# Last output tile: each store as two transfers of 64 rows, one from SyncE and one from ScalarE

## The chip, the cores and the metric

The kernel runs on one core of one Trainium2 chip. The metric is the device time of one execution in microseconds, as the median of several runs. In the text TensorE, VectorE, ScalarE, GpSimd and SyncE are the five engines of the core; the profile calls them PE, DVE, ACT, POOL and SP. SyncE computes nothing: it waits for semaphores and issues transfers (DMAs) between the core's memory (SBUF) and the chip's (DRAM).

## What is computed

For an input x of 2048 rows with 448 columns the kernel computes a gated mix of two branches:

```
g   = sigmoid(x @ gate_w)                        # one number per row
a   = attention(x @ wqkv) @ wo                   # 16 heads of 28; each row looks at 8 rows, 2 apart
b   = relu(x @ w1 + b1)**2 @ w2 + b2             # 448 -> 1792 -> 448
out = g * a + (1 - g) * b
```

Everything is float32. Matrix products are made from a high and a low part of each operand, in three products.

## The kernel before, in words

The 2048 rows are split by parity (`par` 0 and 1), since the attention steps by two, and each parity into eight tiles of 128 rows (`t` 0 to 7). Four chunks of four such tiles go through the matrix products of q, k and v (lines 257 to 298). Then the four chunks go through the other branch in the order 3, 0, 1, 2 (line 50 and the loop at line 1049), while GpSimd and VectorE work on the attention beside it. The order on every engine is written out by the program itself: `advance` (line 478) keeps a planned clock of TensorE and calls what has come due.

A finished tile of the output comes together in SBUF in `bt` tiles of 128 rows by 448 columns. `fin_add` (line 822) adds one branch's sum, scaled by its gate, to such a tile: one VectorE instruction (line 823), then a transfer. If the other branch was already there, the tile goes to the output (line 825); otherwise it goes to a buffer in DRAM (line 831) or is kept. All transfers are issued by SyncE, in the order in which the program asks for them. A transfer counts up one of eight completion semaphores in turn, and the next transfer on the same semaphore first waits for it.

The last work is the product with `wo` for the tiles 6 and 7 of parity 1, in `wo_last` (line 926). Its helper list `outs` has three entries: tile 6 with all 448 columns (r = 0), tile 7 with the first 224 columns, and tile 7 with the last 224 (both r = 1). For each entry nine matmuls run (line 944), then `fin_add` adds and stores (line 946). So the last tile is stored in two halves of 224 columns, 112 KB each, and the second can be issued only when the last nine matmuls and VectorE's add behind them are done. Other lines that the prediction speaks of: 367 (o_d stores of 128 rows), 639 (the first load of the program), 642, 876 and 1004 (loads of 64 rows), 571 (ScalarE's one-column copies).

At the end of the program (line 1165 in the profile) SyncE waits for all completion semaphores and for the other engines' counters, in five waits of two semaphores each. Then all engines meet in a barrier.

Of the kernel before, what the change touches and what calls it, by code (L numbers as in the profile page):

```python
# [13 lines left out]
S, D, H, DH, W, F = 2048, 448, 16, 28, 8, 1792  # L14
P = 128
# [42 lines left out]
def gated_mix_kernel(ctx: ExitStack, tc: tile.TileContext, xT, wqkv, w1, w2, wo, b1, b2, out):  # L58
    nc = tc.nc
# [38 lines left out]
    zt, gt, g1t = zg[:, 0:2], zg[:, 2:4], zg[:, 4:6]  # L98
# [46 lines left out]
    def ps(tag, name):  # L145
        return psum.tile([P, 512], F32, tag=tag, name=name, bufs=4)
# [331 lines left out]
    def advance(dt):  # L478
        clock["pe"] += dt
        while due := [x for x in later if x[0] <= clock["pe"]]:  # L480
            item = min(due, key=lambda x: x[0])
            later.remove(item)
            item[1]()
        if not clock["on"]:
            clock["att"] = clock["pe"]
            return
        while clock["att"] < clock["pe"]:
            try:
                r = next(att)
            except StopIteration:  # L490
                clock["on"] = False
                return
            if r is None:
                clock["att"] = clock["pe"]
                return
            clock["att"] += r
# [300 lines left out]
    fin = {}  # L797
# [21 lines left out]
    def fin_tile(par, t):  # L819
        return ahead.pop((par, t), None) or fin_begin(par, t)  # L820

    def fin_add(par, t, bt, pt, g, cols=slice(0, D)):
        nc.vector.scalar_tensor_tensor(bt[:, cols], pt, g, bt[:, cols], op0=ALU.mult, op1=ALU.add)  # L823
        if (par, t) in fin:
            nc.sync.dma_start(out[par, t, :, cols], bt[:, cols])
            fin[par, t] = "stored"
        elif par == 1 and t < 4:
            ahead[par, t] = bt
            fin[par, t] = "half"
        else:  # L830
            nc.sync.dma_start(f_d[par, t], bt)
            fin[par, t] = "half"
# [3 lines left out]
    def o_part(c, f, second, tls):  # L836

        for tl in tls:
            if f == 0 and not second:
                bps[tl] = Acc("b", f"b{c}_{tl}", D, 6 * NF)  # L840
        todo = []
        for r in range(2):
            tl = tls[(r + f // 2 + second) % 2]
            sl = slice(tl * P, tl * P + P)
            ps = []
            for g in (f + 1, f) if second else (f, f + 1):
                (hh, hl), (wh, wl) = hs[c, g], w2hl(g)
                ps += [(bps[tl], a[:, sl], w) for a, w in (((hl, wh), (hh, wh), (hh, wl)) if second else
                                                           ((hh, wh), (hh, wl), (hl, wh)))]
            todo.append(ps)  # L850
        go(todo, MM448)
        if second and f == NF - 2:
            for tl in tls:
                par, t = c // 2, (c % 2) * 4 + tl
                fin_add(par, t, fin_tile(par, t), bps[tl].pt[:, :D], g1t[:, par, t:t + 1])
# [56 lines left out]
    def wo_three(acc, oh, ol, wh, wl):  # L912
        return [(acc, oh, wh), (acc, oh, wl), (acc, ol, wh)]

    def wo_full(st, r, ks):
        _, _, accs, oh, ol, *_ = st
        return sum((wo_three(accs[r], oh[:, k, r], ol[:, k, r], woh[:, k], wol[:, k]) for k in ks), [])
# [8 lines left out]
    def wo_last(st, between):  # L926


        par, t, accs, oh, ol, o7, o8 = st
        half = D // 2  # L930
        outs = [(0, accs[0].pt, slice(0, D)), (1, accs[1].pt, slice(0, half)),
                (1, ps("b", "last"), slice(half, D))]
        for j, (_, a, w) in enumerate(wo_three(None, o7, o8, wo7h, wo7l)):
            for r, pt, cols in outs:
                rows = slice(r * 64, r * 64 + 64)
                nc.tensor.matmul(pt[:, :cols.stop - cols.start], a[rows], w[rows, cols], start=j == 0, stop=False)  # L936
        advance(3 * MM448)
        between()
        tiles = [fin_tile(par, t + r) for r in range(2)]
        for r, pt, cols in outs:  # L940
            n = cols.stop - cols.start
            todo = wo_full(st, r, (0, 1, 2))
            for j, (_, a, w) in enumerate(todo):
                nc.tensor.matmul(pt[:, :n], a, w[:, cols], start=False, stop=j == len(todo) - 1)  # L944
            advance(9 * MM448 * n / D)
            fin_add(par, t + r, tiles[r], pt[:, :n], gt[:, par, t + r:t + r + 1], cols)

    def wo_second(st):
        par, t, accs, *_ = st
        go([wo_full(st, 1 - r, (2, 0, 1)) for r in range(2)], MM448)  # L950
        for r in range(2):
            fin_add(par, t + r, fin_tile(par, t + r), accs[r].pt[:, :D], gt[:, par, t + r:t + r + 1])
# [161 lines left out]
    for n, (tls, second) in enumerate(((left, False), (right, False), (left, True), (right, True))):  # L1114
        if second:
            o_turn(c, f, tls)
        if n in (1, 2, 3):
            st = at_hand()
            if n == 3:
                wo_last(st, lambda: o_part(c, f, second, tls))  # L1120
                break
            split_now()
            wo_first(st)
        o_part(c, f, second, tls)
        if n in (1, 2):
            wo_second(st)
# [43 lines left out]
```

## Time and profile before

| | us |
|---|---|
| median of 3 runs | 415.18 (414.21 to 415.46) |
| the profiled execution | 414.58 |
| its span, first to last instruction | 412.7 |
| end of the last matmul, from the start of the span | 409.64 |
| issue of the last store begins | 410.14 |

The profile is of one execution. Its times count from the start of the span; the 1.9 us between span and execution lie around it. A row of a transfer (DMA_DIRECT2D, engine SPq) shows how long its issue kept SyncE, not how long the data moved; "to landing" counts from the start of the issue until the completion semaphore has its full count. The granted clock of TensorE was 1.00 throughout.

### The profile page before, as it was taken

To read this page: it belongs to the slowest core of one execution; us is meant where nothing else is said; L and a number is where in the kernel's file an instruction comes from. 1 tells how busy PE (TensorE), PEld (TensorE's weight loads), DVE (VectorE), ACT (ScalarE), POOL (GpSimd) and SP (SyncE) were. 2 spreads that over 40 slices of the span, in tenths; PEclk is the share of its full clock that TensorE was granted. 3 is DMA by queue.
4 is the path that set the end of the run, shared out by engine and by line. 5 is a ranking of instruction groups with operands and counts; after the bars stand their busy time and mean duration, and the time that the engine had idled before them with its cause. 6 is when DMAs were issued, how large, how long until landed. Compare 5 with 4: busy or idle time off the path is not lost.

```text
span 412.7 us, 9323 instructions
## 1 busy us (share of the span) xinstructions
PE 408.4 (99%) x3835; PEld 377.6 (91%) x3835; DVE 255.9 (62%) x404; ACT 211.9 (51%) x477; POOL 268.6 (65%) x167
## 2 busy tenths in 40 slices
PE   8999999999999999999999999999999999999997
PEld 8999999999999999888888888989898888888996
DVE  4520523276767767777656798879576677892354
ACT  5642556378756565444565535444653254346540
POOL 0000000965989999999989899999899977860000
PEclk9999999999999999999999999999999999999999
DMA  7989799989164307654112649765145611168204
GB/s 236 380 318 326 227 364 292 363 259 321 47 224 159 128 2 258 207 186 152 37 50 93 233 157 266 200 149 149 24 163 192 224 46 59 72 175 139 91 0 180
DMA packets 65611, 73.76 MB, mean 179 GB/s; under 512 B 32352, under 2 KB 58528, under 8 KB 65184
## 3 DMA queue, kind: packets, MB, share of 16 engines
q1 hardware_dynamic: 65568, 73.16, 54.5%
q8 instruction: 30, 0.49, 0.5%
q14 instruction: 13, 0.11, 0.1%
HBM read 45.71 MB, written 28.25 MB: 179 GB/s over the span
## 4 chain that ended last, share of the span: by engine, by line
PE 99%; DVE 0%; issue 0%
PE b L188 33%; PE h L188 32%; PE qkv L188 23%; PE a L188 7%; PE qkv L266 2%; PE warm L632 1%; PE a L944 1%; PE last L944 0%; DVE bt L823 0%; PE last L936 0%; PE a L936 0%; DVE zero L629 0%; DVE b1z L630 0%
## 5 line engine op out<-in xcount | busy, mean ns | idle before, releaser
L339 POOL TENSOR_TENSOR qk<-q,k 128x896 f32<-128x896 f32 x64 | 135.0, 2138 | 83.2 <-DMA k<-k_d 78.9
L346 POOL TENSOR_TENSOR av<-lg,v 128x896 f32<-128x896 f32 x64 | 119.5, 1962 | 8.0 <-DVE lg L340 5.6
L188 PE MATMUL qkv<-wqh,x 64*128 64x448 f32 (+1 forms) x528 | 90.9, 360 | 0.0
L619 DVE TENSOR_TENSOR h<-h,h 128x512 fp32r<-128x512 f32 x56 | 38.3, 687 | 60.8 <-ACT h L622 60.4
L188 PEld LDWEIGHTS qkv<-wqh,x 64*128 64x128 f32 x528 | 74.0, 184 | 1.3
L188 PE MATMUL qkv<-wql,x 64*128 64x448 f32 (+1 forms) x264 | 74.7, 360 | 0.0
L188 PE MATMUL b<-w2ah,h 64*128 64x448 f32 x448 | 70.4, 359 | 0.0
L188 PE MATMUL b<-w2bh,h 64*128 64x448 f32 x448 | 69.6, 360 | 0.0
L340 DVE TENSOR_REDUCE lg<-qk 128x32 f32<-128x896 f32 x64 | 67.1, 1076 | 2.2 <-POOL qk L339 2.1
L354 DVE TENSOR_REDUCE o<-av 128x112 f32<-128x896 f32 x64 | 66.5, 1070 | 2.1 <-POOL av L346 1.8
L620 ACT ACTIVATE h<-h,b1z 128x512 f32<-128x512 f32 x56 | 36.7, 656 | 44.0 <-PE h L188 44.0
L188 PEld LDWEIGHTS b<-w2ah,h 64*128 64x128 f32 x448 | 48.0, 184 | 2.8
L188 PEld LDWEIGHTS b<-w2bh,h 64*128 64x128 f32 x448 | 46.0, 184 | 3.2 <-ACT h L571 0.3
L188 PE MATMUL b<-w2al,h 64*128 64x448 f32 x224 | 47.6, 358 | 0.0
L188 PEld LDWEIGHTS qkv<-wql,x 64*128 64x128 f32 x264 | 45.5, 184 | 0.7
L188 PE MATMUL b<-w2bl,h 64*128 64x448 f32 x224 | 45.8, 358 | 0.0
L207 ACT ACTIVATE st<-qkv 128x448 f32<-128x448 f32 x48 | 24.5, 543 | 32.2 <-PE qkv L188 27.1
L188 PE MATMUL h<-x,w1h 64*128 64x512 f32 x168 | 36.1, 386 | 0.0
L621 ACT ACTIVATE h<-h 128x512 fp32r<-128x512 f32 x56 | 33.5, 599 | 1.7
L622 ACT ACTIVATE h<-h 128x512 f32<-128x512 f32 x56 | 33.2, 593 | 0.0
L188 PE MATMUL h<-x,w1l 64*128 64x512 f32 x84 | 29.7, 386 | 0.0
L571 ACT ACTIVATE h<-h 128x4 fp32r<-128x4 f32 (+1 forms) x35 | 7.2, 206 | 42.6 <-PE b L188 42.4
(145 smaller groups left out, 749.4 us busy)
## 6 DMA issues: line engine op xcount, KB each, us to landing
k<-k_d SPq DMA_DIRECT2D x8, 840.0 KB, 6.7
v<-v_d SPq DMA_DIRECT2D x8, 840.0 KB, 4.4
x_d<-x SPq DMA_DIRECT2D x11, 512.0 KB, 6.0
q_d<-st SPq DMA_DIRECT2D x8, 448.0 KB, 4.6
k_d<-st SPq DMA_DIRECT2D x8, 448.0 KB, 4.1
v_d<-st SPq DMA_DIRECT2D x8, 448.0 KB, 7.1
w1raw<-w SPq DMA_DIRECT2D x4, 896.0 KB, 10.0
q<-q_d SPq DMA_DIRECT2D x8, 448.0 KB, 3.6
```

Source lines behind the costliest of these rows:

```text
L188: nc.tensor.matmul(acc.pt[:, :acc.n], a[rows], w[rows], start=acc.todo == acc.all, stop=acc.todo == 1)
L207: nc.scalar.activation(st[:, :, t % 2], pt[:, :D].rearrange("p (g c) -> p g c", g=G), AF.Copy)
L266: nc.tensor.matmul(acc.pt[:, :NQ], a, w, start=k == j == 0, stop=False)
L339: nc.gpsimd.tensor_mul(pr, q[:, s:s + 1].to_broadcast([P, W, C]), k[:, s:s + W])
L340: pending.append(lambda: nc.vector.tensor_reduce(lg[:, s], pr.rearrange("p w (h d) -> p w h d", h=HG), axis=AX.X, op=ALU.add))
L346: nc.gpsimd.tensor_mul(pr.rearrange("p (h d) w -> p w h d", h=HG), lg[:, s][:, :, :, None].to_broadcast([P, W, HG, DH]), v[:, s:s + W].rea ...
L354: nc.vector.tensor_reduce(o[:, g * C:(g + 1) * C], pr, axis=AX.X, op=ALU.add)
L571: nc.scalar.activation(ap, f32(ap), AF.Copy)
L619: nc.vector.tensor_sub(hl, pt, f32(hh))
L620: ops += [lambda pt=pt, r=r: nc.scalar.activation(pt, pt, AF.Relu, bias=b1t[:, f + r:f + r + 1]), lambda pt=pt, hh=hh: nc.scalar.activatio ...
L621: lambda pt=pt, hh=hh: nc.scalar.activation(hh, pt, AF.Square),
L622: lambda pt=pt, r=r, low=low: (nc.scalar.activation(pt, pt, AF.Square), at(delays[r], low))]
```

## The change

`fin_add` gets a flag, `two`. `wo_last` passes `r`, so that it is set for the two column halves of tile 7 and for nothing else. With the flag, the store of a half goes as two transfers: rows 0 to 63 issued by SyncE and rows 64 to 127 issued by ScalarE, 56 KB each. The rest of the program is as it was.

```diff
-    def fin_add(par, t, bt, pt, g, cols=slice(0, D)):
+    def fin_add(par, t, bt, pt, g, cols=slice(0, D), two=False):
         nc.vector.scalar_tensor_tensor(bt[:, cols], pt, g, bt[:, cols], op0=ALU.mult, op1=ALU.add)
-        if (par, t) in fin:
+        if two:
+            for e, rows in ((nc.sync, slice(0, 64)), (nc.scalar, slice(64, P))):
+                e.dma_start(out[par, t, rows, cols], bt[rows, cols])
+            fin[par, t] = "stored"
+        elif (par, t) in fin:
             nc.sync.dma_start(out[par, t, :, cols], bt[:, cols])
             fin[par, t] = "stored"
...
-            fin_add(par, t + r, tiles[r], pt[:, :n], gt[:, par, t + r:t + r + 1], cols)
+            fin_add(par, t + r, tiles[r], pt[:, :n], gt[:, par, t + r:t + r + 1], cols, r)
```

## The prediction

> **What bounds the kernel now.** I read four views of the profiled execution of the kernel before, from the outside in: the page for the whole span, the chain that ended last for its last microseconds, the timeline of the same stretch, and SyncE's own waits.
>
> ```profile
> span 412.7 us, 9323 instructions
> PE 408.4 (99%) x3835; PEld 377.6 (91%) x3835; DVE 255.9 (62%) x404; ACT 211.9 (51%) x477; POOL 268.6 (65%) x167
> PE 99%; DVE 0%; issue 0%
> ```
>
> TensorE (PE) is busy for 408.4 of 412.7 us and 99% of the chain runs on it. The change touches no matmul, and the order of instructions on TensorE, VectorE and GpSimd is the same in both kernels. So nothing can be won or lost but in what follows the last matmul. The chain of the last 8 us, and the timeline from 409.5 us, show where that begins:
>
> ```profile
> 408.62 1.02 PE last L944 x9
> 409.64 0.02 issue
> 409.66 0.45 DVE bt L823
> ...
> 410.14 0.33 SPq L825 DMA_DIRECT2D out<-bt  x1
> ```
>
> In the first three rows the columns are start, length, what. The last matmul ends at 409.64, VectorE adds its result into the output tile until 409.66 + 0.45 = 410.11, and SyncE (SP) begins to issue the last store at 410.14. The chain as printed stops at 410.11, because it follows instructions and not transfers; the span goes on to 412.7. Those last 2.6 us are the whole field of this change. What SyncE waits for in them (total, times, longest), and how busy the 16 DMA engines are (last two columns: their share, and GB/s):
>
> ```profile
> SPq L1165 <- DMA out<-bt: 0.8, 1, 0.8
> SPq L1165 <- PEq L1165: 0.6, 2, 0.4
> ...
> 410.45:410.95 0.50, 0.00 (x0) 0.00 (x0) 0.00 (x0) 0.00 (x0) 0.00 (x0) 1.00 0.00 0
> 410.95:411.50 0.55, 0.00 (x0) 0.00 (x0) 0.00 (x0) 0.00 (x0) 0.00 (x0) 1.00 0.66 209
> 411.50:411.95 0.45, 0.00 (x0) 0.00 (x0) 0.00 (x0) 0.00 (x0) 0.00 (x0) 1.00 0.05 18
> ```
>
> So the tail has five pieces: the issue (0.33), a gap without traffic until about 410.95, the packets until about 411.5, their confirmation until the landing at 410.14 + 1.7 = 411.84 (the 1.7 is quoted below), and then the closing barrier of all engines up to 412.7. SyncE waits 0.8 us for that store with nothing else to do: the landing of the last store sets the end.
>
> **The change part by part.** The output tile for r = 1 is stored in two column halves. I call them A (first 224 columns, begun at 409.1) and B (last 224 columns, begun at 410.14). Each now goes as two transfers of 64 rows: A1 and B1 from SyncE, A2 and B2 from ScalarE. By the order lists SyncE still issues two transfers there, ScalarE two more, each behind one wait.
>
> *The issue.* Rows of all transfers of a line: least, median, longest duration in ns, first and last start. The first two lines move 128 rows per transfer, the last three 64 rows.
>
> ```profile
> L367 SPq DMA_DIRECT2D o_d<-o x16: 319/320/602, 230.9 to 369.6; - x16
> L825 SPq DMA_DIRECT2D out<-bt x17: 332/338/1357, 270.5 to 410.1; - x17
> ...
> L1004 SPq DMA_DIRECT2D woraw<-wo_d x2: 497/542/587, 189.4 to 189.9; - x2
> L642 SPq DMA_DIRECT2D wqraw<-wqkv x2: 572/579/586, 4.0 to 4.6; - x2
> L876 SPq DMA_DIRECT2D ot<-o_d x16: 612/617/837, 248.0 to 380.1; - x16
> ...
> SPq L1004 <- ACT h L621: 0.4, 1, 0.4
> ...
> L825 SPq DMA_DIRECT2D out<-bt x1: 332/332/332, 410.1 to 410.1; - x1
> DMA to landing us min/median/max: 1.7/1.7/1.7
> ```
>
> Half the rows doesn't mean half the issue: all 20 transfers of 64 rows took 0.50 to 0.84 us to issue, while a store of 128 rows takes 0.32 to 0.34 as a rule. The nearest row is the 0.497: it is a 64-row transfer that, like B1, came straight after a wait for a compute engine (the wait is the row of L1004 on ScalarE's h); the others stood in a rush of issues. I take 0.50 in place of 0.33: **+0.17 us**. From below, if the cost went with the rows, it would be 0.17 instead of 0.33, −0.17; from above, with the longest row, 0.84, +0.50. Nothing hides this: the issue begins when VectorE is done and the packets follow it. For A1 and A2 it is hidden: they begin at 409.1 and B at 410.14, so an issue of up to about 0.97 us is covered by VectorE's wait for the last matmuls and its add; above that, B starts late by the excess.
>
> ScalarE has issued no transfer in the trace of before. Its last instruction is long done:
>
> ```profile
> 400.88 0.19 ACT L571 ACTIVATE h<-h 128x2 fp32r<-128x2 f32 x1
> ...
> L639 SPq DMA_DIRECT2D wqraw<-wqkv x1: 391/391/391, 0.7 to 0.7; - x1
> ...
> L825 SPq DMA_DIRECT2D out<-bt x1: 1357/1357/1357, 404.5 to 404.5; - x1
> DMA to landing us min/median/max: 3.5/3.5/3.5
> ```
>
> No work of ScalarE stands behind A2 and B2, so nobody waits for what is queued there but the closing barrier. The bounds for an issue by ScalarE are 0.33 (a 128-row store of SyncE) and 1.36 (the longest store issue in this trace). I take SyncE's 0.50, because SyncE's very first issue, the second row, cost only 0.39: a queue's first use is not dear there. The waits put ahead of the four transfers are for earlier transfers that used the same completion semaphore. The latest of those is the store issued at 404.5, which lands 3.5 us later at 408.0, a microsecond before A begins: 0.
>
> *The packets.* Two sizes of 128-row stores have a time to landing:
>
> ```profile
> out<-bt SPq DMA_DIRECT2D x15, 224.0 KB, 2.0
> out<-bt SPq DMA_DIRECT2D x2, 112.0 KB, 1.7
> ```
>
> Half the bytes land 0.3 us earlier; halving once more, to 56 KB, would give about 0.15. That is the most that smaller transfers can win. But B1 and B2 come out together and the same 112 KB must be moved: the 0.66 share between 410.95 and 411.50 is all 16 DMA engines at work on them. I take **0**, with −0.15 as the other end. The Trainium skill, page "DMA: Bandwidth & Descriptors", section "Rules for kernel authors", speaks against this change: two transfers to disjoint halves of the partitions serialise, since both spread over the same engines, whether one engine issues them or two, so one 128-partition transfer is better. By it this term is 0, as taken; by the two sizes alone it would be −0.15. No run here shows two queues at once.
>
> A moves too: its packets come about 0.17 later, into the stretch from 410.45 to 410.95, whose share of 0.00 shows that it is free.
>
> *The closing waits.* Before the barrier SyncE checks all completion semaphores in five waits:
>
> ```profile
> L1165 SPq EVENT_SEMAPHORE  x5: 27/28/28, 410.5 to 411.9; - x5
> ...
> L1165 SPq EVENT_SEMAPHORE  x3: 27/28/28, 410.9 to 411.0; - x3
> ...
> L1165 SPq EVENT_SEMAPHORE  x1: 28/28/28, 411.9 to 411.9; - x1
> ```
>
> Before, four pass between 410.5 and 411.0 while the last store is under way, and only the fifth, at 411.9, is held by it. In the changed program B1's and B2's semaphores are named in the second and third wait, so two or three waits are left to pass after the landing. The three from 410.9 to 411.0 make two steps in some 0.1 us, about 0.07 a step: two or three steps are 0.14 to 0.2. I take **+0.15**, with 0 and 0.3 as ends. What follows (the barrier, 0.8 us) is unchanged.
>
> *The sum*: +0.17 + 0 + 0.15 = +0.32 us, rounded to +0.35 for the second issuer. The profiled execution took 414.58 us, of which 1.9 lie around its span of 412.7; with the change 414.93. The median of the three runs, 415.18, is 0.60 above the profiled one, so I forecast **415.5 us** for the median. 0.3% of this kernel is 1.25 us, which is also what its three runs spread over (414.21 to 415.46): about what a measurement can tell from no change. The forecast is **no change that can be told**.
>
> **The rivals.**
>
> *The two issues take turns.* If SyncE and ScalarE cannot generate transfers at the same time, B2 starts when B1's issue is over. For it: back-to-back issues on SyncE never overlap. Against it: those are one engine's, and no row shows two. Price: a second 0.50 in line, less the 0.15 because the last train is then half as long: +0.35 more, in all +0.7, 415.9 us. The Trainium skill, page "Perfetto Trace Analysis", section "DMA Instruction — HWDGE (DVE, Sync)", says that the block that generates descriptors is shared between issuing sequencers and locked for one at a time; by that this rival would be the case, and no run here shows it.
>
> *The halves do win.* The issue costs no more than before (0.33) and each train is half as long: −0.15 and the closing waits +0.15, in all 0; with the issue at half, −0.17: 415.0 to 415.2. Against it: 20 of 20 rows with 64 rows are slower to issue.
>
> *ScalarE is a slow issuer* (the other side: slower). The mechanism is two ScalarE issues of length I in line, A2 from about 409.14 and B2 behind it. Up to I = 0.96 A2 is covered and only B2 counts: I − 0.33. Above, B2 ends at 409.18 + 2I in place of 410.47, so 2I − 1.29, less 0.15 for the half train, plus 0.15 for the closing waits. It costs more than 1.25 us from I = 1.27 on; at the 1.36 row it is +1.43, 416.6 us, and at 1.6 it would be +1.9, 417.1. For it: nothing in the trace shows ScalarE issue, and SyncE itself has issues that long. Against it: the median of SyncE's 17 stores is 0.34.
>
> *It doesn't do what it says* is as good as excluded by the order lists; left is a shift in the program's code that moves some wait unseen.
>
> **How the numbers follow.** The forecast (both halves side by side, 415.2 to 415.8) has 0.42; the issues in turn 0.20; the halves win 0.12; the slow ScalarE 0.24; anything else 0.02. Slower by over 0.3% (above 416.4): most of the slow ScalarE, 0.20, and 0.08 from the two milder losses where the spread of runs adds to them: 0.28. Faster by over 0.3% (below 413.9): no case reaches it, since from the end of the last add to the landing there are only 1.7 us and at most 0.3 of them could go; 0.05 for the spread of runs. Within 0.3%: 0.67. The range goes from 414.3 (the best case, −0.3, in a run as quick as the quickest shown) to 417.0 (the slow ScalarE nearly to its end).
>
> **What would show it.** Right, if the profile after has issues of 0.45 to 0.65 us for both B1 and B2, begun within 0.1 us of each other; one train of packets of about 0.5 us beginning some 1.0 us after the issue begins; a landing 0.1 to 0.25 us later than the 1.7 of before; and two or three of SyncE's five closing waits after it. Wrong, if B2's issue begins or ends after B1's by the length of an issue (turns), if a row of ScalarE shows over 1.2 us (slow issuer), if the landing comes before 1.7 us (the halves win), or if anything before 409 us moved.

## The result, and the profile after

| | before | after |
|---|---|---|
| median of 22 runs each, us | 414.56 (414.11 to 415.86) | 415.49 (414.9 to 417.69) |
| ratio to before | 1 | 1.0024 (95% interval 1.0016 to 1.0033) |
| the profiled execution, us | 414.58 | 415.25 |

The change costs about 1.0 us (0.7 to 1.4 by the interval). With 22 runs of each kernel that is clear of no change, though it is below 0.3%.

The page of the kernel after shows four instructions more (two waits and two transfers of ScalarE) and a second queue, q10, ScalarE's, beside SyncE's q1. Its columns are packets, MB, and share of the DMA engines.

```profile
span 413.5 us, 9327 instructions
...
q10 hardware_dynamic: 160, 0.11, 0.1%
```

The 160 packets are two transfers of 64 rows with 16 completion marks each. The end of the chain of the kernel after (start, length, what):

```profile
408.55 1.02 PE last L949 x9
409.57 0.02 issue
409.59 0.45 DVE bt L823
```

The last add ends at 409.59 + 0.45 = 410.04, against 410.11 before. In these two executions nothing was lost ahead of the last store; the tail behind the last add grew from 2.61 to 3.43 us. Its first piece, the two issues of half B:

```profile
L827 SPq DMA_DIRECT2D out<-bt x1: 496/496/496, 410.1 to 410.1; - x1
L827 ACTq DMA_DIRECT2D out<-bt x1: 511/511/511, 410.1 to 410.1; - x1
```

They stand side by side, half a microsecond each, and begin 4 ns apart; the one before took 0.332. The landings, from the DMA page of the same stretch (last column, us after the issue began):

```profile
out<-bt SPq DMA_DIRECT2D x1, 56.0 KB, 1.9
out<-bt ACTq DMA_DIRECT2D x1, 56.0 KB, 2.3
```

The store of before took 1.7 to land. Both halves are later than that, with half the bytes, and ScalarE's is later by 0.35 than SyncE's, although both issues ran at the same time. The packets say why. From 411.19 to 411.48 only SyncE's queue moves:

```profile
q1 hardware_dynamic: 55, 0.05, 75.4%
```

from 411.49 to 411.64 both move:

```profile
q10 hardware_dynamic: 26, 0.02, 60.4%
q1 hardware_dynamic: 22, 0.01, 21.2%
```

and from 411.66 to 411.93 ScalarE's queue and a code load (q14, kind instruction):

```profile
q10 hardware_dynamic: 47, 0.03, 48.2%
q14 instruction: 1, 0.01, 10.1%
```

The second transfer starts in its turn, 0.28 behind the first, and is still under way when the first is done; the issue rows show nothing of it. This late start is what the text calls a turn. Behind the landing, SyncE's closing waits:

```profile
L1170 SPq EVENT_SEMAPHORE  x3: 28/28/299, 412.1 to 412.5; - x3
L1170 SPq DRAIN  x2: 7/7/7, 412.5 to 412.6; - x2
```

The 299 ns is the wait that ScalarE's landing ends (at 412.34); two more follow. Last, the barrier. ScalarE's DRAIN in the kernel after, and in the kernel before:

```profile
L1170 ACTq DRAIN  x1: 135/135/135, 413.1 to 413.1; - x1
```

```profile
L1165 ACTq DRAIN  x1: 14/14/14, 412.3 to 412.3; - x1
```

Before, it began 0.1 us after the ScalarE wait ahead of it (412.2); after, 0.35 later than its wait (412.8), and all engines waited for it.

For all kernels of this study, from the records of the traces, in us after the end of the last add: when the first data packet of each queue's part of half B starts, when the last part has landed, and then how long the closing waits and the barrier took. Landing, closing waits and barrier add up to the tail. Of x1, x2, x3 and x7 to x10 there is one execution each, the profiled one, so that only the tail is used of them.

| kernel | SyncE's packets | ScalarE's packets | last landing | closing waits | barrier | tail |
|---|---|---|---|---|---|---|
| before | 0.85 | | 1.76 | 0.09 | 0.76 | 2.61 |
| after | 1.17 | 1.45 | 2.29 | 0.19 | 0.94 | 3.43 |
| x1: rows 0-63 by SyncE alone | 1.22 | | 2.05 | 0.09 | 0.76 | 2.90 |
| x2: rows 64-127 by ScalarE alone | | 1.24 | 2.74 | 0.09 | 0.76 | 3.59 |
| x9: rows 0-63 by ScalarE alone | | 1.24 | 2.73 | 0.09 | 0.76 | 3.58 |
| x3: both by SyncE | 1.49, 2.31 | | 3.17 | 0.25 | 0.76 | 4.18 |
| x7: 16 columns of B | 1.18 | 1.45 | 2.04 | 0.19 | 0.94 | 3.18 |
| x6: only B in halves | 1.22 | 1.50 | 2.35 | 0.09 | 0.76 | 3.20 |
| x4: halves by columns | 0.85 | 1.00 | 1.81 | 0.19 | 0.94 | 2.94 |
| x5: B whole by ScalarE | | 0.90 | 1.84 | 0.09 | 0.76 | 2.69 |
| x8: after, two copies more | 1.18 | 1.45 | 2.23 | 0.19 | 0.76 | 3.18 |
| x10: before, four copies more | 0.85 | | 1.73 | 0.09 | 0.94 | 2.76 |
| x12: both cut 96 and 32 | 0.84 | 1.18 | 1.99 | 0.19 | 0.94 | 3.12 |
| x11: only B cut 96 and 32 | 0.87 | 1.21 | 2.01 | 0.09 | 0.76 | 2.86 |

After against before: landing +0.54, closing waits +0.10, barrier +0.18, together +0.82.

### The profile page after: what moved, and what is told of

The parts are those of the page before. It is cut to its first block, busy times and chain, and to the rows that moved or that the text cites. A ratio compares the mean times of both kernels' runs of the same rounds, so it can differ in the third digit from the quotient of the medians.

```text
span 413.5 us, 9327 instructions
## 1 busy us (share of the span) xinstructions
PE 408.1 (99%) x3835; PEld 374.9 (91%) x3835; DVE 255.9 (62%) x404; ACT 211.9 (51%) x477; POOL 268.4 (65%) x167
## 4 chain that ended last, share of the span: by engine, by line
PE 97%; DMA 1%; SPq 0%; DVE 0%; ACT 0%; issue 0%
PE b L188 33%; PE h L188 32%; PE qkv L188 23%; PE a L188 7%; PE qkv L266 1%; DMA xraw<-xT 1%; PE a L949 1%; PE last L949 0%; SPq L644 0%; SPq L639 0%; DVE bt L823 0%; ACT x L662 0%; PE last L941 0%; PE a L941 0%
## 5 line engine op out<-in xcount | busy, mean ns | idle before, releaser
L188 PE MATMUL b<-w2bh,h 64*128 64x448 f32 x448 | 68.6, 360 | 0.0
L188 PE MATMUL b<-w2bl,h 64*128 64x448 f32 x224 | 44.9, 358 | 0.0
L188 PE MATMUL h<-x,w1h 64*128 64x512 f32 x168 | 35.2, 386 | 0.0
L188 PE MATMUL h<-x0b,w1h 64*128 64x512 f32 x168 | 28.1, 386 | 0.0
```

Source lines behind the costliest of these rows:

```text
L188: nc.tensor.matmul(acc.pt[:, :acc.n], a[rows], w[rows], start=acc.todo == acc.all, stop=acc.todo == 1)
```

## The experiments

Three theories for the late landing: **G**, the two transfers take turns where transfers are generated (a descriptor, in the expectations, is the order for one packet); **E**, they take turns because the DMA engines or the memory's ports are busy with the first one; **S**, ScalarE's queue is slower by itself. Diffs are against the changed kernel, inside `if two:`, unless another kernel is named.

### x1: rows 0 to 63 by SyncE alone

```diff
-            for e, rows in ((nc.sync, slice(0, 64)), (nc.scalar, slice(64, P))):
-                e.dma_start(out[par, t, rows, cols], bt[rows, cols])
+            if cols.start:
+                nc.sync.dma_start(out[par, t, 0:64, cols], bt[0:64, cols])
+            else:
+                nc.sync.dma_start(out[par, t, :, cols], bt[:, cols])
```

> Half A goes as in the kernel before (one SyncE transfer of 128 rows). Of half B only rows 0 to 63 are stored, by SyncE alone; rows 64 to 127 of B are left out, and ScalarE issues nothing. If the two transfers take turns where they are generated (theory G) or at the DMA engines (theory E), and SyncE's is first in line, the lone one looks like B1 of the changed kernel: issue about 0.50 us, landing 1.9 us after it. If B1 was slowed by its companion, it lands earlier, at about 1.75. ScalarE's closing DRAIN is as early as in the kernel before.

Its row of the last issue, and the landing:

```profile
L827 SPq DMA_DIRECT2D out<-bt x1: 539/539/539, 409.8 to 409.8; - x1
...
DMA to landing us min/median/max: 2.0/2.0/2.0
```

Alone, with half the bytes, it lands 0.3 us later than the whole store of before (1.7). SyncE's half in the changed kernel (1.9) landed no later with its companion than this one alone. A store of 64 rows has a cost of its own: the issue is 0.2 longer and the packets start 0.37 later (table: 1.22 against 0.85).

### x2 and x9: one half by ScalarE alone

As x1, with `nc.scalar` and rows 64 to 127 (x2) or 0 to 63 (x9).

> The mirror image: half A as in the kernel before, of half B only rows 64 to 127 are stored, by ScalarE alone; rows 0 to 63 of B are left out. Theories G and E: without the companion there is no turn to wait for, landing about 1.9 us after the issue in place of 2.26. Theory S (ScalarE's queue is slower by itself): 2.2 to 2.3 us as in the changed kernel.

> Of half B only rows 0 to 63 are stored, by ScalarE alone; rows 64 to 127 are left out. The run with the upper rows landed 2.70 us after its issue, because one of its 16 completion marks came 0.41 after the others while an 8 KB code load was under way on the same engines. If that is the whole of it and ScalarE's queue is not slower by itself, this one lands at 2.0 us, as SyncE's lone transfer of the same rows did (2.02), unless a code load meets it again. Theory S: 2.2 or more with all 16 marks late.

Both landed at 2.7, where S would have it. But x9 shows that this isn't the queue. Its issue and landing, then its queues from 411.40 to 412.25, then from 411.85 to 412.30:

```profile
L827 ACTq DMA_DIRECT2D out<-bt x1: 555/555/555, 410.2 to 410.2; - x1
...
DMA to landing us min/median/max: 2.7/2.7/2.7
```

```profile
q10 hardware_dynamic: 80, 0.06, 29.4%
q14 instruction: 1, 0.01, 4.9%
```

```profile
q10 hardware_dynamic: 5, 0.00, 2.4%
```

80 packets are the whole transfer, 64 rows and 16 marks. Five of them are left after 411.85: four rows and one mark, a sixteenth of the transfer. The other 15 marks are written by 1.65 us after the last add, as SyncE's are in x1 (1.63), and the packets start at 1.24 against 1.22. Beside the store ran an 8 KB code load that began at 1.245 and took 0.66 us; the first of the four late rows starts at 1.905, within 4 ns of the load's end, and in x2 it is the same (1.912 and 1.915). So S is refuted for the queue, and the late sixteenth, 0.4 us, is put down to the code load. That is argued from these two coincidences; no run takes the load away, and in x5 such a load, begun at 1.287 beside ScalarE's store, held up no row. I had expected x9 to escape it. The load came at the same moment in both.

### x7: 16 of 224 columns

```diff
+            few = slice(cols.start, cols.start + 16) if cols.start else cols
             for e, rows in ((nc.sync, slice(0, 64)), (nc.scalar, slice(64, P))):
-                e.dma_start(out[par, t, rows, cols], bt[rows, cols])
+                e.dma_start(out[par, t, rows, few], bt[rows, few])
```

> As the changed kernel, but of half B only 16 of the 224 columns are stored (64 bytes a row in place of 896), by both engines; the other 208 columns of B are left out. Theory G: the number of descriptors is the same, so ScalarE's transfer still trails by 0.25 to 0.35 us in its landing. Theory E (the engines or the memory's ports are busy with the first transfer): packets are a small part of 896 bytes, so the trailing falls below 0.1 us.

Landings, then the queues from 411.65 to 411.92, then from 411.92 to 412.20:

```profile
out<-bt SPq DMA_DIRECT2D x1, 4.0 KB, 1.7
out<-bt ACTq DMA_DIRECT2D x1, 4.0 KB, 2.0
```

```profile
q1 hardware_dynamic: 80, 0.00, 16.7%
```

```profile
q10 hardware_dynamic: 80, 0.00, 16.0%
```

All 80 packets of SyncE's queue, then all 80 of ScalarE's, with the engines 83 to 84% idle throughout, and 0.1 us without a packet of either queue in between. The trail is 0.34 us with 64 bytes a row, as it was with 896. So the DMA engines are not what the second transfer waits for: E falls, G stands. That the generation of the transfer is what they take turns at is the step left over; no row shows it directly.

### x3: both halves by SyncE

```diff
-            for e, rows in ((nc.sync, slice(0, 64)), (nc.scalar, slice(64, P))):
-                e.dma_start(out[par, t, rows, cols], bt[rows, cols])
+            for rows in (slice(0, 64), slice(64, P)):
+                nc.sync.dma_start(out[par, t, rows, cols], bt[rows, cols])
```

> Both halves of rows, of A and of B, are issued by SyncE, one behind the other. Issue 0.50 to 0.60 us each, the second beginning about 0.55 after the first. If turns at the generator are what costs (G), the second transfer follows the first by its issue and lands about 0.55 + 1.9 = 2.4 to 2.5 us after the first issue begins, 0.1 to 0.2 later than in the changed kernel (2.26). If ScalarE's queue is slow by itself (S), two transfers on one queue are no worse than 2.26.

```profile
L827 SPq DMA_DIRECT2D out<-bt x4: 475/536/597, 409.6 to 411.8; - x4
```

One queue is worse, and by more than I had expected: the last landing is 2.86 after B1's issue began, not 2.4 to 2.5. A's two issues kept SyncE until 0.2 after the last add, so B1 began 0.28 late, and B2's issue began 0.34 after B1's had ended, a gap with no wait; without the gap it would be 2.52. This speaks against S, but it does not test G, since on one engine B2's issue begins after B1's under any theory. ScalarE as second issuer does save time against that.

### x6: only half B in two

```diff
+            if cols.start:
                 for e, rows in ((nc.sync, slice(0, 64)), (nc.scalar, slice(64, P))):
                     e.dma_start(out[par, t, rows, cols], bt[rows, cols])
+            else:
+                nc.sync.dma_start(out[par, t, :, cols], bt[:, cols])
```

> Only half B is split; half A is one SyncE transfer as in the kernel before. ScalarE issues one transfer. By the completion semaphores in turn, ScalarE's B2 now sits in the fifth and last closing wait and B1 in the third. Theory: the turn (B2 lands about 0.53 us later than the store of before) stays, the two closing waits behind the landing (0.10 us) go, so the tail is about 0.1 shorter than that of the changed kernel, +0.5 to +0.75 us over before. Rival: if the split of A were part of the cost (A's trains pushing B's), the tail would fall by 0.3 or more.

```profile
out<-bt SPq DMA_DIRECT2D x1, 56.0 KB, 2.0
out<-bt ACTq DMA_DIRECT2D x1, 56.0 KB, 2.3
```

The landing stays as late (2.35), the closing waits go back to 0.09, and so does the barrier to 0.76, which I had not expected. The tail is 3.20, +0.59 over before. So splitting A had no part in the late landing. The time, 1.003 (1.0019 to 1.0042), is no better than the changed kernel's.

### x4 and x5: 128 rows by both, and by ScalarE alone

```diff
-            for e, rows in ((nc.sync, slice(0, 64)), (nc.scalar, slice(64, P))):
-                e.dma_start(out[par, t, rows, cols], bt[rows, cols])
+            for e, o in ((nc.sync, 0), (nc.scalar, 112)):
+                half = slice(cols.start + o, cols.start + o + 112)
+                e.dma_start(out[par, t, :, half], bt[:, half])
```

> Each half goes as two transfers of 128 rows by 112 columns, one by SyncE and one by ScalarE: the same bytes and issuers, no 64-row transfer. If 64 rows are what makes the issue slow, both issues fall from 0.50 to about 0.33 (SyncE; 0.33 to 0.45 for ScalarE). Theory G: the second still waits for its turn, now behind 128 descriptors, and trails by 0.3 us or more; B2 lands 2.1 to 2.4 us after the issue. Without turns: both land at about 1.75 and the tail is that of before plus 0.1 for closing waits.

The same bytes from the same two engines, with no transfer of 64 rows:

```profile
L828 ACTq DMA_DIRECT2D out<-bt x2: 366/370/375, 409.2 to 410.2; - x2
...
L828 SPq DMA_DIRECT2D out<-bt x1: 332/332/332, 410.2 to 410.2; - x1
```

```profile
out<-bt SPq DMA_DIRECT2D x1, 56.0 KB, 1.6
out<-bt ACTq DMA_DIRECT2D x1, 56.0 KB, 1.8
```

The issue is back at 0.33 and 0.37, the packets start at 0.85, and ScalarE's trail by 0.15 only, less than I gave for a turn. The last landing is 0.06 later than before, where the change's is 0.54 later: most of the late landing, 0.48, goes with the 64-row transfers. The other 0.28 of x4's tail are closing waits and barrier, as in the changed kernel. Its time is 1.0006 (0.9997 to 1.0014) of before. The 0.15 behind 128 rows, against 0.28 behind 64, says something on G too: the wait for the turn doesn't grow with the number of descriptors ahead, as I had assumed. What sets its length stays open.

x5 is `(nc.scalar if cols.start else nc.sync).dma_start(out[par, t, :, cols], bt[:, cols])`.

> Half A as before by SyncE, half B as one transfer of 128 rows by ScalarE: the change of issuer alone, with no split. If ScalarE's queue is no slower (against S): issue 0.33 to 0.45 us, landing 1.7 to 1.9 us, time within 0.2 us of before except for ScalarE's closing DRAIN, which I expect about 0.35 late, as in the changed kernel (+0.18 us on the end). Theory S: landing at 2.0 or more.

```profile
L826 ACTq DMA_DIRECT2D out<-bt x1: 371/371/371, 410.6 to 410.6; - x1
...
DMA to landing us min/median/max: 1.7/1.7/1.8
```

The landing of 1.8 is B's, the 1.7 A's: ScalarE is a normal issuer. The closing DRAIN was not late here, against my expectation. The time was 1.001 (1.0001 to 1.0018) of before.

### x8 and x10: the late DRAIN

x8 adds two one-element copies on ScalarE to the changed kernel, ahead of the loop over `outs`; x10 adds four to the kernel before.

```diff
         tiles = [fin_tile(par, t + r) for r in range(2)]
+        for _ in range(2):
+            nc.scalar.activation(none, none, AF.Copy)
         for r, pt, cols in outs:
```

> The changed kernel with two one-element copies more on ScalarE, done while it idles before the last stores. Nothing else differs. In the changed kernel ScalarE's second closing DRAIN came 0.35 us late and the barrier took 0.94 in place of 0.76 us. If that hangs on where the instruction stands in ScalarE's stream (four instructions were added ahead of it), two more move the place and the barrier falls back to 0.76, the tail from 3.43 to about 3.25. If it is a cost of having two transfers in flight from ScalarE, it stays at 0.94.

> The kernel before with four one-element copies on ScalarE, done while it idles, and no transfer on ScalarE: as many instructions as the change adds to it. If the late DRAIN hangs on the place in the stream, it appears here too, without any split: barrier 0.94 in place of 0.76 us, the rest of the tail as before (landing 1.75 after the last add). If it is a cost of transfers on ScalarE, the barrier stays at 0.76.

The DRAIN of x8, then of x10 and the wait ahead of it:

```profile
L1172 ACTq DRAIN  x1: 8/8/8, 413.1 to 413.1; - x1
```

```profile
L1167 ACTq EVENT_SEMAPHORE  x2: 17/17/17, 414.5 to 415.2; - x2
L1167 ACTq DRAIN  x1: 127/127/127, 414.9 to 414.9; - x1
```

x8 has two transfers on ScalarE and a barrier of 0.76; x10 has none and a barrier of 0.94. The 0.18 us hangs on the place of one instruction in ScalarE's stream, and is not a cost of transfers. The table fits: the kernels with four instructions added to ScalarE's stream (after, x4, x7, x10, x12) have 0.94, those with none, two or six (x8) have 0.76. Why that place is late, no row shows.

### x12 and x11: cut 96 and 32

```diff
-            for e, rows in ((nc.sync, slice(0, 64)), (nc.scalar, slice(64, P))):
+            for e, rows in ((nc.sync, slice(0, 96)), (nc.scalar, slice(96, P))):
```

x11 has the same cut in x6's form.

> The change itself with another cut: rows 0 to 95 from SyncE and 96 to 127 from ScalarE, in both halves. Same number of transfers, issuers, waits and instructions. If it is having fewer than 128 rows that makes issue and start slow, both transfers look like those of 64 rows: issue about 0.50, first packets 1.15 us after it, tail 3.3 to 3.5 after the last add. If it is the 64-row form in particular, the issues fall to 0.33 to 0.37, the first packets come at 0.83 and about 0.15 later for the second in turn, the last landing 1.75 to 1.85, tail 2.9 to 3.0 (before 2.61, of the rest 0.10 closing waits and 0.18 late DRAIN), and the time is that of before plus 0.1 to 0.5 us.

> Only half B is cut 96 to 32; A is one transfer as before. Against the run that cut only B 64 to 64 (tail 3.20, no closing wait and no late DRAIN behind the landing): with fewer rows at fault the tail stays at 3.1 to 3.2; with the 64-row form at fault it is 2.6 to 2.7, within 0.1 us of before. It is the best version that the runs point to, and I expect it to be no faster than before, since the same 112 KB still leave after the same last add.

The last issues and landings of x11:

```profile
L828 SPq DMA_DIRECT2D out<-bt x1: 349/349/349, 410.2 to 410.2; - x1
L828 ACTq DMA_DIRECT2D out<-bt x1: 407/407/407, 410.2 to 410.2; - x1
```

```profile
out<-bt SPq DMA_DIRECT2D x1, 84.0 KB, 1.8
out<-bt ACTq DMA_DIRECT2D x1, 28.0 KB, 2.0
```

96 rows start like 128 (0.84 in x12, 0.87 in x11), so fewer than 128 rows isn't what is dear by itself; of the cuts tried, the late start of the first part comes with 64 rows alone. The second part still trails, by 0.34, more than I had expected, so the tails are 3.12 and 2.86: better than 64 and 64 in the same form (3.43 and 3.20), worse than before. Whether the 32 rows waited for a turn or start late by themselves stays open; they weren't run alone. The times are 1.0019 (1.001 to 1.0028) and 1.0012 (1.0 to 1.0024). No version of the split beat the kernel before.

## Why the prediction was right, and where it was wrong

The range (414.3 to 417.0) held the time, and within 0.3% came true (0.24%). That 415.5 met 415.49 is luck: the forecast added 0.35 to a median of three runs, 415.18, where 22 runs have 414.56. The change itself was forecast at +0.35 and is about +1.0; "no change that can be told" was wrong for this many runs. The lower end of the range is not what its words say either: the quickest run shown, 414.21, less 0.3 is 413.9; the 414.3 comes from the profiled 414.58. Of the four signs that I had named for being right, two came (the issue rows, the number of closing waits) and two did not: the packets took 0.70 us in two staggered trains in place of one of about 0.5, and the landing was 0.53 later in place of 0.1 to 0.25.

- *The field is the last 2.6 us*: right. The last add ended at 410.11 before and 410.04 after.
- *The issue, 0.50 for a half, ScalarE's the same*: right (0.496 and 0.511).
- *That it costs +0.17*: too small. The step let the packets move with the issue's length. They began 1.145 us after SyncE's issue began, against 0.826 before: +0.32, and +0.37 for the lone transfer of x1.
- *The packets, 0*: this step failed. It had B1 and B2 come out together. ScalarE's packets began 0.28 after SyncE's; the half-length train gave back 0.08. 0.32 + 0.28 − 0.08 makes 0.52 of the 0.54 by which the landing moved. Why a 64-row transfer starts late, and why the second waits, no row shows; x1, x4, x7 and x12 show what they do and do not hang on.
- *The closing waits, +0.15*: right (0.10; two waits were left).
- *The barrier, unchanged*: wrong by 0.18, by four instructions more ahead of ScalarE's DRAIN. The order lists show those four; I had priced only what they do.
- *The rivals*: "the two issues take turns" had 0.20 and +0.7, and the outcome is nearest to it. The sign that I named for it, B2's issue row beginning or ending late, was not there: the turn showed in the packets alone. By the Trainium skill, page "Perfetto Trace Analysis", section "DMA Instruction — HWDGE (DVE, Sync)", the generator's lock wait is part of the profiled row; here ScalarE's row beside SyncE's is 0.511, no longer than ScalarE's row alone (0.556 in x2), so the wait of 0.28 is not in the row. If a shared generator makes the turns of x7, its wait lies behind the row, and not where that page of the Trainium skill has it. "The halves do win" falls with x1, "ScalarE is a slow issuer" with x5.

One thing stays open. The tails explain +0.82, +0.59, +0.33, +0.08, +0.52 and +0.25 us for after, x6, x4, x5, x12 and x11; the ratios say +1.0, +1.2, +0.25, +0.4, +0.8 and +0.5 (of 414.6). Each tail lies within its interval but that of x6, whose interval begins at +0.79; yet five of the six ratios say more than the tail. Each tail is of one execution, and I have not settled whether a kernel with transfers on ScalarE loses something elsewhere too.

## What to carry to other kernels

A transfer at the very end of a kernel is paid from its issue to its landing, and cutting it in two can only help if the part that lands last lands earlier than the whole would: check in the packets of each queue, not in the issue rows, whether two transfers run side by side. Cut by columns over all 128 rows rather than in two times 64 rows, and compare with one transfer first. Count every instruction that is put on an idle engine's stream, and look which of the closing waits the new transfers come to stand in.

## What the runs showed of the hardware that I had not expected

- The last tile's stores of 64 rows took 0.48 to 0.60 us to issue and, where they were not second of two issued at once, 1.13 to 1.25 from the issue's start until their first packet, from either engine; those of 128 or 96 rows 0.32 to 0.38 and 0.81 to 0.87.
- Two stores issued at the same time from two engines started to move one after the other, 0.13 to 0.35 us apart; with 64 rows it was 0.27 to 0.28 with 64 bytes a row as with 896 (x7).
- Packets of 896 bytes took 41 to 45 ns on average in these stores of 128 and 32 rows, and 54 to 63 in those of 64 and 96.
- The 14 profiled executions differ in the first 15 us: line 188 begins between 12.4 and 15.1. From the first matmul of line 188 to the last add all have 397.4 to 397.6 us. The chain's start in the kernel before and in x10, whose neighbouring run of the kernel before was as slow (417.07):

```profile
1.20 3.14 PE warm L632 x13
4.33 8.42 PE qkv L266 x36
12.76 7.28 PE qkv L188 x67
```

```profile
1.20 3.42 DMA xraw<-xT
...
5.08 10.08 PE qkv L266 x36
15.16 4.88 PE qkv L188 x43
```

In x10 the first matmuls wait for the load of x and the matmuls of line 266 take until 15.16 in place of 12.76. A single run thus says nothing about an effect of a microsecond, while the tail behind the last add, read from one profile, tells 0.1: the landing of the same last transfers differed by 0.02 between before and x10, and by 0.07 between after and x8.
